# A gated recurrence and a highway layer on one core: short units at both ends of the token loop, and the weight loads moved on ScalarE's queue

## The chip, the cores and the metric

The kernel runs on one NeuronCore of a Trainium2 chip. The metric is the device time of one execution in microseconds, as the median of repeated runs. Besides these there is one profiled execution, whose trace gives the start and the duration of every instruction; its own time is a little different from the median.

## What is computed

A recurrence over 6336 tokens for each of 4 batches and 256 channels, and then a highway layer on each of the 25344 resulting rows (everything float32 in memory):

```python
sig = 1 / (1 + exp(-f_logit))
f = lower_bound + (1 - lower_bound) * sig
for t in range(S):                       # B, S, D = 4, 6336, 256
    h = f[:, t] * h + (1 - f[:, t]) * x[:, t]
    y[:, t] = h
H = maximum(y @ w_h, 0)
T = sigmoid(y @ w_t + b_t)
out = T * H + (1 - T) * y
```

The kernel writes u = sigmoid(-f_logit) and cc = 1 - lower_bound. Then 1 - f = cc * u and f = 1 - cc * u. The scan runs on u * x without the factor cc, and cc is put back into the weights (scaled rows) and into a diagonal matrix used for the output.

## The kernel before

**Units.** Tokens are cut into units, and the kernel is a software pipeline over them. 6336 = 6 x 1024 + 192. Unit 0 holds the first 192 tokens of all four batches: 8 blocks of 96 tokens on 96 partitions (`rest // 2`), so 768 columns. Units 1 to 24 each hold 1024 tokens of one batch, 8 blocks of 128, going round the four batches for each stretch of 1024. `units` (L48 to L51) lists them, and `load` (L67), `gate` (L116), `halves` (L166) and `o_act` (L227) read their sizes.

**Stages of a unit n.** There are two halves h (or m) of 128 channels, and the steps are made for each:

- `load`: logits into `lt`, x into `xt`, both on SP's queue. Four buffers each.
- `gate` (L119): ScalarE, u = sigmoid(-lt), one instruction for the whole unit.
- `product` (L126): GpSimd, bv = u * x, in pieces of two blocks (128x512). The first piece is told to wait for the e of unit n - 3 on VectorE.
- `decay_pe`, `decay_act` (L136, L144): TensorE transposes u so that channels lie on partitions; ScalarE turns it into f.
- `b_pe` (L150): TensorE transposes bv.
- `scan` (L161): VectorE, y = f * y + bv along the tokens; for unit 0 four scans of 192, one a batch, otherwise one of 1024. The last column is carried on.
- `z_pe`, `t_act` (L175, L183): y @ w_t, then the sigmoid with the bias.
- `g_pe`, `d_dve`, `e_dve` (L190, L199, L206 or L209): y @ (cc w_h - cc I), then d = max(-cc y, .), which is max(H, 0) - h, and e = d * T.
- `o_pe`, `o_act` (L223, L224, L233): y times the diagonal plus e, transposed back to tokens on partitions in groups of four blocks; ScalarE copies each group from PSUM and SP stores it (L237, or L241 for unit 0).

**Order.** The order on every engine is written out by hand: `pin` keeps an instruction in program order on its engine. In iteration n of the loop (L247 to L291) stand the load of unit n + 4, the gate and product of n + 2, the decay of n + 1, the scans of n, t, d and e of n - 1, and the output of n - 2. On VectorE that gives scan(n,0), d(n-1,0), scan(n,1), d(n-1,1), e(n-1). Every PSUM tile (uT, bT, zp, gp, op) has one buffer. Output tiles have two.

**Head.** SP issues the loads of units 0 and 1. ScalarE's queue carries lower_bound and the bias in four small transfers, and then w_h and w_t of 256 KB each (L96, L99), all ahead of its first activation. VectorE makes cc, the scaled weights `w_sb` and the diagonal (L101 to L113) before its first scan.

Of the kernel before, what the change touches and what calls it, by code (L numbers as in the profile page):

```python
# [19 lines left out]
def kernel(  # L20
# [21 lines left out]
    NB = 8  # L42
    out_bsd = out.rearrange("(b s) d -> b s d", b=B)


    rest = S % (NB * P)
    assert rest % 2 == 0 and rest // 2 <= P and B * 2 == NB
    units = [(rest // 2, [(b, 0, b * rest, rest) for b in range(B)])]  # L48
    for s0 in range(rest, S, NB * P):
        for b in range(B):  # L50
            units.append((P, [(b, s0, 0, NB * P)]))  # L51
# [14 lines left out]

    def load(n):  # L67
        np_, segs = units[n]
        lt = inp.tile([P, NB, D], FP32, tag="lt")
        xt = inp.tile([P, NB, D], FP32, tag="xt")  # L70
        for src, t in ((f_logit, lt), (x, xt)):
            if len(segs) == 1:
                b, s0, _, ln = segs[0]
                pin(nc.sync.dma_start(t, src[b, s0:s0 + ln, :].rearrange("(j p) d -> p j d", p=np_)))
            else:
                t4 = t.rearrange("p (b j) d -> p b j d", j=2)
                for j in range(2):
                    nc.sync.dma_start(
                        t4[:np_, :, j, :],
                        src[:, j * np_:(j + 1) * np_, :].rearrange("b p d -> p b d"))  # L80
        st[n]["lt"], st[n]["xt"] = lt, xt

    load(0)
# [7 lines left out]
    lb = singles.tile([P, NH], FP32, name="lb")  # L91
    bt = singles.tile([P, NH], FP32, name="bt")
    w_raw = singles.tile([P, 2, NH, D], FP32, name="w_raw")
    for h in range(NH):
        for vec, t in ((lower_bound, lb), (moe_b_t, bt)):
            nc.scalar.dma_start(t[:, h:h + 1], bass.AP(  # L96
                tensor=vec.tensor, offset=vec.offset + h * P, ap=[[1, P], [1, 1]]))
    for k, w in enumerate((moe_w_h, moe_w_t)):
        nc.scalar.dma_start(w_raw[:, k], w.rearrange("(h p) o -> p h o", p=P))  # L99
# [7 lines left out]
    for h in range(NH):  # L107
        for k in range(2):
            nc.vector.tensor_scalar(w_sb[:, k, h], w_raw[:, k, h], cc[:, h:h + 1], None, op0=ALU.mult)
        nc.vector.tensor_scalar(diag[:, h], ident_h, cc[:, h:h + 1], None, op0=ALU.mult)  # L110
        nc.vector.tensor_scalar(ndiag[:, h], ident_h, ncc[:, h:h + 1], None, op0=ALU.mult)

        nc.vector.scalar_tensor_tensor(w_sb[:, 0, h, h * P:(h + 1) * P], w_raw[:, 0, h, h * P:(h + 1) * P],  # L113
                                       cc[:, h:h + 1], ndiag[:, h], op0=ALU.mult, op1=ALU.add)

    def gate(n):  # L116
        np_, _ = units[n]
        u = inp.tile([P, NB, D], FP16, tag="u")
        pin(nc.scalar.activation(u[:np_], st[n]["lt"][:np_], AF.Sigmoid, scale=-1.0))  # L119
        st[n]["u"] = u  # L120

    def product(n, after):
        np_, _ = units[n]
        bv = mid.tile([P, NB, D], BF16, tag="bv")
        for q in range(0, NB, 2):
            ins = pin(nc.gpsimd.tensor_mul(bv[:np_, q:q + 2], st[n]["u"][:np_, q:q + 2], st[n]["xt"][:np_, q:q + 2]))  # L126
            if q == 0 and after is not None:
                tc.add_manual_dep(ins.ins, after.ins.name, mybir.DependencyInfo(
                    mybir.DependencyClass.Sync, mybir.DependencyReason.DATA), reason="shared port")
        st[n]["bv"] = bv  # L130

    def decay_pe(n, h):
        np_, _ = units[n]
        uT = ps1.tile([P, NB * P], FP16, tag="uT")
        for j in range(NB):
            pin(nc.tensor.transpose(uT[:, j * np_:(j + 1) * np_], st[n]["u"][:np_, j, h * P:(h + 1) * P], ident_h[:np_, :np_]))  # L136
        st[n]["uT"] = uT

    def decay_act(n, h):
        np_, _ = units[n]  # L140
        N = NB * np_
        if h == 0:
            st[n]["f"] = mid.tile([P, NH, NB * P], FP16, tag="f", name="f")
        pin(nc.scalar.activation(st[n]["f"][:, h, :N], st[n]["uT"][:, :N], AF.Identity, scale=ncc[:, h:h + 1], bias=1.0))  # L144

    def b_pe(n, h):
        np_, _ = units[n]
        bT = ps1.tile([P, NB * P], BF16, tag="bT")
        for j in range(NB):
            pin(nc.tensor.transpose(bT[:, j * np_:(j + 1) * np_], st[n]["bv"][:np_, j, h * P:(h + 1) * P], ident_b[:np_, :np_]))  # L150
        st[n]["bT"] = bT
# [3 lines left out]
    def scan(n, h):  # L155
        if h == 0:
            st[n]["y"] = ypool.tile([P, NH, NB * P], BF16, tag="y", name="y")
        y = st[n]["y"]
        for b, _, c0, ln in units[n][1]:
            prev = carry.get((b, h))  # L160
            pin(nc.vector.tensor_tensor_scan(  # L161
                y[:, h, c0:c0 + ln], st[n]["f"][:, h, c0:c0 + ln], st[n]["bT"][:, c0:c0 + ln],
                0.0 if prev is None else prev, op0=ALU.mult, op1=ALU.add))
            carry[b, h] = y[:, h, c0 + ln - 1:c0 + ln]

    def halves(n):  # L166
        N = NB * units[n][0]
        return [(0, N // 2), (N // 2, N)]

    def z_pe(n, m):  # L170
        zp = ps1.tile([P, 2, 512], FP32, tag="zp")
        y = st[n]["y"]
        for ki in range(NH):
            for i, (a, e) in enumerate(halves(n)):
                pin(nc.tensor.matmul(zp[:, i, :e - a], w_sb[:, 1, ki, m * P:(m + 1) * P], y[:, ki, a:e],  # L175
                                 start=ki == 0, stop=ki == NH - 1))
        st[n]["zp"] = zp

    def t_act(n, m):
        w = NB * units[n][0] // 2  # L180
        if m == 0:
            st[n]["t"] = ffn.tile([P, NH, 2, 512], BF16, tag="t", name="t")
        pin(nc.scalar.activation(st[n]["t"][:, m, :, :w], st[n]["zp"][:, :, :w], AF.Sigmoid, bias=bt[:, m:m + 1]))  # L183

    def g_pe(n, m):
        gp = ps1.tile([P, 2, 512], FP32, tag="gp")
        y = st[n]["y"]
        for ki in range(NH):
            for i, (a, e) in enumerate(halves(n)):
                pin(nc.tensor.matmul(gp[:, i, :e - a], w_sb[:, 0, ki, m * P:(m + 1) * P], y[:, ki, a:e],  # L190
                                 start=ki == 0, stop=ki == NH - 1))
        st[n]["gp"] = gp

    def d_dve(n, m):
        w = NB * units[n][0] // 2
        if m == 0:
            st[n]["d"] = ffn.tile([P, NH, 2, 512], BF16, tag="d", name="d")
        y2 = st[n]["y"][:, m, :2 * w].rearrange("p (i w) -> p i w", i=2)
        pin(nc.vector.scalar_tensor_tensor(st[n]["d"][:, m, :, :w], y2, ncc[:, m:m + 1], st[n]["gp"][:, :, :w],  # L199
                                       op0=ALU.mult, op1=ALU.max))  # L200

    def e_dve(n):
        w = NB * units[n][0] // 2
        e = mid.tile([P, NH, 2, 512], BF16, tag="e", name="e")
        if w == 512:
            ins = pin(nc.vector.tensor_mul(e, st[n]["d"], st[n]["t"]))  # L206
        else:
            for m in range(NH):
                ins = pin(nc.vector.tensor_mul(e[:, m, :, :w], st[n]["d"][:, m, :, :w], st[n]["t"][:, m, :, :w]))  # L209
        st[n]["e"] = e  # L210
        return ins

    def o_pe(n, q):
        np_, _ = units[n]
        w = NB * np_ // 2
        op = ps1.tile([P, NB // 2, D], FP32, tag="op")
        y, e = st[n]["y"], st[n]["e"]
        for jj in range(NB // 2):
            j = q * (NB // 2) + jj
            i, c = divmod(j * np_, w)  # L220
            for h in range(NH):
                o = op[:np_, jj, h * P:(h + 1) * P]
                pin(nc.tensor.matmul(o, y[:, h, j * np_:(j + 1) * np_], diag[:, h], start=True, stop=False))  # L223
                pin(nc.tensor.matmul(o, e[:, h, i, c:c + np_], ident_b, start=False, stop=True))  # L224
        st[n]["op"] = op

    def o_act(n, q):  # L227
        np_, segs = units[n]
        if q == 0:
            st[n]["o"] = outp.tile([P, NB, D], FP32, tag="o", name="o")  # L230
        o = st[n]["o"]
        oq = o[:, q * (NB // 2):(q + 1) * (NB // 2)]
        pin(nc.scalar.copy(oq[:np_], st[n]["op"][:np_]))  # L233
        if len(segs) == 1:
            b, s0, _, ln = segs[0]
            a = s0 + q * (ln // 2)
            nc.sync.dma_start(out_bsd[b, a:a + ln // 2, :].rearrange("(j p) d -> p j d", p=np_), oq)  # L237
        elif q == 1:
            o4 = o.rearrange("p (b j) d -> p b j d", j=2)
            for j in range(2):  # L240
                nc.sync.dma_start(out_bsd[:, j * np_:(j + 1) * np_, :].rearrange("b p d -> p b d"),  # L241
                                  o4[:np_, :, j, :])
# [4 lines left out]
    for n in range(-3, NU + 2):  # L247
# [21 lines left out]
        if ok(n):  # L269
            scan(n, 1)  # L270
        if ok(n - 1):
# [3 lines left out]
        if ok(n - 2):  # L275
# [44 lines left out]
```

## Time and profile before

| quantity | us |
|---|---|
| median of three runs (lowest, highest) | 236.33 (235.71, 237.41) |
| the profiled run | 237.56 |
| its span, first to last instruction | 235.8 |
| first scan starts | 16.48 |
| first scan of unit 2 starts | 31.65 |
| last e ends | 226.78 |
| last copy of output ends | 231.90 |

Busy time of the engines in that span: VectorE 203.6 us (86%), ScalarE 198.3 (84%), TensorE 192.1 (81%), GpSimd 114.2 (48%). 78.68 MB were moved, 334 GB/s over the span.

How to read it: the page cuts the span into 40 slices and gives the busy tenths of each engine in each. The timeline gives instructions with their start, their duration and, in brackets, the idle time of the engine just before and what ended it. The chain of waits follows back from the last instruction what released what. A share of busy time is a mean over the head, the middle and the tail, which have different limits; it is the stage that has to be read.

### The profile page before, as it was taken

To read this page: it belongs to the slowest core of one execution; us is meant where nothing else is said; L and a number is where in the kernel's file an instruction comes from. 1 tells how busy PE (TensorE), PEld (TensorE's weight loads), DVE (VectorE), ACT (ScalarE), POOL (GpSimd) and SP (SyncE) were. 2 spreads that over 40 slices of the span, in tenths; PEclk is the share of its full clock that TensorE was granted. 3 is DMA by queue.
4 is the path that set the end of the run, shared out by engine and by line. 5 is a ranking of instruction groups with operands and counts; after the bars stand their busy time and mean duration, and the time that the engine had idled before them with its cause. 6 is when DMAs were issued, how large, how long until landed. Compare 5 with 4: busy or idle time off the path is not lost.

```text
span 235.8 us, 4853 instructions
## 1 busy us (share of the span) xinstructions
PE 192.1 (81%) x2000; PEld 134.5 (57%) x2000; DVE 203.6 (86%) x144; ACT 198.3 (84%) x176; POOL 114.2 (48%) x108
## 2 busy tenths in 40 slices
PE   0135899898999989899998989898999989897751
PEld 0125566666566666667566666656666666665441
DVE  0425799999999999999999999999999999999540
ACT  0645789999999999999999999999999999975541
POOL 1088553574376357436634753673475357430000
PEclk9999999999999999999999999999999999999985
DMA  6999999999999999999999999999999995243255
GB/s 150 302 386 386 386 383 386 379 385 383 382 386 383 386 382 386 384 384 379 386 386 382 385 383 383 379 382 375 385 383 386 388 368 205 97 152 119 89 178 177
DMA packets 78805, 78.68 MB, mean 334 GB/s; under 512 B 2240, under 2 KB 78784, under 8 KB 78784
## 3 DMA queue, kind: packets, MB, share of 16 engines
q1 hardware_dynamic: 77664, 77.86, 94.4%
q10 hardware_dynamic: 1120, 0.53, 0.9%
q8 instruction: 15, 0.25, 0.4%
q14 instruction: 6, 0.05, 0.0%
HBM read 52.43 MB, written 25.95 MB: 332 GB/s over the span
## 4 chain that ended last, share of the span: by engine, by line
DVE 77%; issue 6%; PE 5%; ACT 2%; DVEq 0%; ACTq 0%
DVE y L161 45%; DVE d L199 20%; DVE e L206 12%; PE zp L175 1%; PE gp L190 1%; ACT o L233 1%; ACT t L183 1%; PE op L224 1%; PE op L223 1%; PE bT L150 0%; PE uT L136 0%; DVE e L209 0%; DVEq L206 0%; ACTq L233 0%; DVEq L209 0%
## 5 line engine op out<-in xcount | busy, mean ns | idle before, releaser
L126 POOL TENSOR_TENSOR bv<-u,xt 128x512 bf16<-128x512 f16 (+1 forms) x100 | 113.2, 1164 | 93.7 <-DVE e L206 72.9
L161 DVE TENSOR_TENSOR_SCAN y<-f,y,bT 128x1024 bf16<-128x1024 f16 x48 | 112.3, 2341 | 2.6 <-ACT t L183 1.4
L183 ACT ACTIVATE t<-zp,bt 128x1024 bf16<-128x1024 f32 (+1 forms) x50 | 55.3, 1106 | 13.6 <-PE zp L175 10.6
L199 DVE SCALAR_TENSOR_TENSOR d<-y,ncc,gp 128x1024 bf16<-128x1024 bf16 (+1 forms) x50 | 62.2, 1244 | 2.5 <-PE gp L190 2.5
L144 ACT ACTIVATE f<-uT,ncc 128x1024 f16<-128x1024 f16 (+1 forms) x50 | 55.9, 1117 | 5.5 <-PE uT L136 5.5
L233 ACT COPY o<-op 128x1024 f32<-128x1024 f32 (+1 forms) x50 | 50.2, 1005 | 5.7 <-PE op L224 5.7
L190 PE MATMUL gp<-y,w_sb 128*128 128x512 bf16 (+1 forms) x200 | 51.5, 380 | 4.0 <-DVE d L199 1.4
L223 PE MATMUL op<-diag,y 128*128 128x128 f16 (+1 forms) x400 | 50.9, 221 | 2.2 <-ACT o L233 2.2
L175 PE MATMUL zp<-y,w_sb 128*128 128x512 bf16 (+1 forms) x200 | 51.6, 381 | 0.3 <-ACT t L183 0.3
L224 PE MATMUL op<-ident_b,e 128*128 128x128 bf16 (+1 forms) x400 | 50.8, 221 | 0.5 <-DVE e L206 0.5
L119 ACT ACTIVATE u<-lt 128x2048 f16<-128x2048 f32 (+1 forms) x25 | 47.5, 1902 | 2.1 <-DMA lt<-in_f_logit_dram 2.1
L150 PE MATMUL bT<-ident_b,bv 128*128 128x128 bf16 (+1 forms) x400 | 31.7, 222 | 20.8 <-DVE y L161 16.5
L224 PEld LDWEIGHTS <-e 128*128 128x128 bf16 (+1 forms) x400 | 39.7, 100 | 8.8 <-DVE e L206 1.9
L223 PEld LDWEIGHTS <-y 128*128 128x128 bf16 (+1 forms) x400 | 39.8, 100 | 5.7
L150 PEld LDWEIGHTS <-bv 128*128 128x128 bf16 (+1 forms) x400 | 26.8, 99 | 27.5 <-issue 20.0
L136 PE MATMUL uT<-ident_h,u 128*128 128x128 f16 (+1 forms) x400 | 32.2, 227 | 11.0 <-ACT u L119 10.0
L190 PEld LDWEIGHTS <-w_sb 128*128 128x128 f16 x200 | 19.6, 98 | 24.4 <-issue 7.1
L136 PEld LDWEIGHTS <-u 128*128 128x128 f16 (+1 forms) x400 | 26.0, 103 | 11.4 <-ACT u L119 10.0
L206 DVE TENSOR_TENSOR e<-d,t 128x2048 bf16<-128x2048 bf16 x24 | 29.4, 1225 | 2.9 <-DVE d L199 0.5
L175 PEld LDWEIGHTS <-w_sb 128*128 128x128 f16 x200 | 18.7, 99 | 18.2 <-issue 1.1
L161 DVE TENSOR_TENSOR_SCAN y<-f,bT 128x192 bf16<-128x192 f16 x8 | 3.8, 534 | 7.3 <-PE bT L150 7.3
L119 ACT ACT_TABLE_LOAD x1 | 1.3, 1283 | 6.7 <-DMA lt<-in_f_logit_dram 6.7
(15 smaller groups left out, 5.7 us busy)
## 6 DMA issues: line engine op xcount, KB each, us to landing
lt<-in_f_logit_dram SPq DMA_DIRECT2D x24, 1024.0 KB, 9.3
xt<-in_x_dram SPq DMA_DIRECT2D x24, 1024.0 KB, 10.6
out_dram<-o SPq DMA_DIRECT2D x48, 512.0 KB, 7.9
lt<-in_f_logit_dram SPq DMA_DIRECT2D x2, 384.0 KB, 5.0
xt<-in_x_dram SPq DMA_DIRECT2D x2, 384.0 KB, 5.7
out_dram<-o SPq DMA_DIRECT2D x2, 384.0 KB, 6.6
w_raw<-in_moe_w_h_dram ACTq DMA_DIRECT2D x1, 256.0 KB, 4.8
w_raw<-in_moe_w_t_dram ACTq DMA_DIRECT2D x1, 256.0 KB, 5.4
```

The source lines that it names most:

```text
L126: ins = pin(nc.gpsimd.tensor_mul(bv[:np_, q:q + 2], st[n]["u"][:np_, q:q + 2], st[n]["xt"][:np_, q:q + 2]))
L136: pin(nc.tensor.transpose(uT[:, j * np_:(j + 1) * np_], st[n]["u"][:np_, j, h * P:(h + 1) * P], ident_h[:np_, :np_]))
L144: pin(nc.scalar.activation(st[n]["f"][:, h, :N], st[n]["uT"][:, :N], AF.Identity, scale=ncc[:, h:h + 1], bias=1.0))
L150: pin(nc.tensor.transpose(bT[:, j * np_:(j + 1) * np_], st[n]["bv"][:np_, j, h * P:(h + 1) * P], ident_b[:np_, :np_]))
L161: pin(nc.vector.tensor_tensor_scan(y[:, h, c0:c0 + ln], st[n]["f"][:, h, c0:c0 + ln], st[n]["bT"][:, c0:c0 + ln], 0.0 if prev is None else ...
L175: pin(nc.tensor.matmul(zp[:, i, :e - a], w_sb[:, 1, ki, m * P:(m + 1) * P], y[:, ki, a:e], start=ki == 0, stop=ki == NH - 1))
L183: pin(nc.scalar.activation(st[n]["t"][:, m, :, :w], st[n]["zp"][:, :, :w], AF.Sigmoid, bias=bt[:, m:m + 1]))
L190: pin(nc.tensor.matmul(gp[:, i, :e - a], w_sb[:, 0, ki, m * P:(m + 1) * P], y[:, ki, a:e], start=ki == 0, stop=ki == NH - 1))
L199: pin(nc.vector.scalar_tensor_tensor(st[n]["d"][:, m, :, :w], y2, ncc[:, m:m + 1], st[n]["gp"][:, :, :w], op0=ALU.mult, op1=ALU.max))
L206: ins = pin(nc.vector.tensor_mul(e, st[n]["d"], st[n]["t"]))
L223: pin(nc.tensor.matmul(o, y[:, h, j * np_:(j + 1) * np_], diag[:, h], start=True, stop=False))
L224: pin(nc.tensor.matmul(o, e[:, h, i, c:c + np_], ident_b, start=False, stop=True))
```

## The change

The list of units has other sizes. The first 192 tokens become two units of two batches each: 4 blocks of 96 tokens on 96 partitions, 384 columns, two scans of 192 for each half. The first 1024 tokens of batch 0 become two units of 512, and the last 1024 tokens of batch 3 become units of 512, 256 and 256. There are 29 units in place of 25, of which 22 have 1024 tokens. Every stage takes the number of blocks from the unit. A unit with up to four blocks has one output group.

On the head: a one-column sigmoid on a zeroed tile stands ahead of everything on ScalarE. lower_bound is one transfer. The two weight loads (w_t first) and the bias are issued on ScalarE's queue behind the gate of unit 0. The scaling of the weights on VectorE stands behind the two scans of unit 0, as one instruction for both matrices of a half, plus the one that subtracts the diagonal. The diagonals are still made at the start.

```diff
+    FIRST, LAST = (4, 4), (4, 2, 2)
...
-    units = [(rest // 2, [(b, 0, b * rest, rest) for b in range(B)])]
+    for b in range(0, B, 2):
+        units.append((rest // 2, 4, [(b, 0, rest), (b + 1, rest, rest)], slice(b, b + 2), 0))
     for s0 in range(rest, S, NB * P):
         for b in range(B):
-            units.append((P, [(b, s0, 0, NB * P)]))
+            last = s0 + NB * P == S and b == B - 1
+            a = s0
+            for nb in (LAST if last else FIRST if not b and s0 == rest else (NB,)):
+                units.append((P, nb, [(b, 0, nb * P)], b, a))
+                a += nb * P
...
+    def pieces(n, dram, t, j0, j1):
+
+        np_, nb, _, b, a = units[n]
+        if isinstance(b, int):
+            return [(dram[b, a + j0 * P:a + j1 * P, :].rearrange("(j p) d -> p j d", p=P), t[:, j0:j1])]
+        t4 = t[:np_, :nb].rearrange("p (b j) d -> p b j d", j=2)
+        return [(dram[b, a + j * np_:a + (j + 1) * np_, :].rearrange("b p d -> p b d"), t4[:, :, j]) for j in range(2)]
...
+    warm = singles.tile([P, 1], FP32, name="warm")
+    nc.gpsimd.memset(warm, 0.0)
+    nc.scalar.activation(warm, warm, AF.Sigmoid)
+
+    lb = singles.tile([P, NH], FP32, name="lb")
+    bt = singles.tile([P, NH], FP32, name="bt")
+    w_raw = singles.tile([P, 2, NH, D], FP32, name="w_raw")
+    nc.scalar.dma_start(lb, lower_bound.rearrange("(h p) -> p h", p=P))
     load(0)
     load(1)
...
-    for h in range(NH):
-        for vec, t in ((lower_bound, lb), (moe_b_t, bt)):
-            nc.scalar.dma_start(t[:, h:h + 1], bass.AP(
-                tensor=vec.tensor, offset=vec.offset + h * P, ap=[[1, P], [1, 1]]))
-    for k, w in enumerate((moe_w_h, moe_w_t)):
-        nc.scalar.dma_start(w_raw[:, k], w.rearrange("(h p) o -> p h o", p=P))
...
+    def load_weights():
+        for k, w in enumerate((moe_w_t, moe_w_h)):
+            pin(nc.scalar.dma_start(w_raw[:, 1 - k], w.rearrange("(h p) o -> p h o", p=P)))
+        pin(nc.scalar.dma_start(bt, moe_b_t.rearrange("(h p) -> p h", p=P)))
+
+    def weights():
+        for h in range(NH):
+            pin(nc.vector.tensor_scalar(w_sb[:, :, h], w_raw[:, :, h], cc[:, h:h + 1], None, op0=ALU.mult))
+
+            pin(nc.vector.scalar_tensor_tensor(
+                w_sb[:, 0, h, h * P:(h + 1) * P], w_raw[:, 0, h, h * P:(h + 1) * P], cc[:, h:h + 1], ndiag[:, h],
+                op0=ALU.mult, op1=ALU.add))
...
+    def spans(n):
+        N = units[n][0] * units[n][1]
+        return [(a, min(a + 512, N)) for a in range(0, N, 512)]
...
         if ok(n):
             scan(n, 1)
+        if n == 0:
+            weights()
         if ok(n - 1):
             g_pe(n - 1, 1)
         if ok(n + 2):
             gate(n + 2)
-        if ok(n - 2):
+        if n + 2 == 0:
+            load_weights()
+        if ok(n - 2) and units[n - 2][1] > QB:
             o_pe(n - 2, 1)
             o_act(n - 2, 1)
```

`QB` is half of `NB`, 4 blocks. In the functions left out, the fixed 8 blocks are replaced by the unit's own number and the fixed halves of a unit by pieces of up to 512 columns.

## The prediction

> **What bounds the kernel now.** First the page's slices: where an engine is full, and where it is not.
>
> ```profile
> PE   0135899898999989899998989898999989897751
> ...
> DVE  0425799999999999999999999999999999999540
> ACT  0645789999999999999999999999999999975541
> ...
> GB/s 150 302 386 386 386 383 386 379 385 383 382 386 383 386 382 386 384 384 379 386 386 382 385 383 383 379 382 375 385 383 386 388 368 205 97 152 119 89 178 177
> ```
>
> VectorE is full from about the sixth slice (5.9 us each) to the third from the end. Two things are not full: the head and the tail. The data rate stands at 375 to 388 GB/s in nearly the whole middle. The windows of the trace give the stages (start:end, then length, busy us of PE, PE weight loads, DVE, ACT, POOL, PE clock, DMA share, GB/s):
>
> ```profile
> 0.00:31.65 31.65, 13.14 (x108) 9.54 (x109) 13.93 (x26) 16.13 (x13) 14.64 (x20) 1.00 1.01 326
> 31.65:211.01 179.36, 164.74 (x1760) 115.39 (x1758) 176.69 (x110) 171.22 (x154) 99.60 (x88) 1.00 1.02 360
> ...
> 220.34:231.90 11.56, 7.46 (x76) 5.33 (x73) 3.78 (x4) 6.17 (x6) 0.00 (x0) 0.84 0.46 163
> 231.90:235.80 3.90, 0.00 (x0) 0.00 (x0) 0.00 (x0) 0.00 (x1) 0.00 (x0) 0.50 0.38 134
> ```
>
> In the middle VectorE is busy 98.5% (176.69 of 179.36). The chain of waits says the same: one period holds both scans, both d, one e, and no other engine.
>
> ```profile
> 162.74 2.26 DVE y L161
> 165.00 0.72 DVE d L199
> 165.72 0.36 issue
> 166.09 2.34 DVE y L161
> 168.43 1.18 DVE d L199
> 169.70 1.23 DVE e L206
> 170.93 2.26 DVE y L161
> ```
>
> Scan to scan is 8.19 us a unit. The scan at 31.65 us is unit 2's first; the e that ends at 220.34 is unit 23's: 23 periods, 188.7 us, 8.20 each. The span is **31.65 head + 188.7 packed VectorE + 11.6 last hand-offs + 3.9 last store = 235.8**. The profiled run took 237.56, so 1.76 lie outside the span; it is 1.2 above the median of 236.33.
>
> Transfers are a near second: a unit moves two loads and a store of 1024 x 256 x 4 bytes, 3.146 MB, and in 8.2 us that is 384 GB/s. They have a lead, though. Unit 22's logits are issued at 164.09 and land about 9.3 later (median of their row), and their gate is at 183.95: 10.5 us of slack.
>
> The head in the timeline:
>
> ```profile
> 6.71 1.28 ACT L119 ACT_TABLE_LOAD   x1 [6.71 <-DMA lt<-in_f_logit_dram]
> ...
> 11.46 4.52 POOL L126 TENSOR_TENSOR bv<-u,xt 96x512 bf16<-96x512 f16 x4 [9.80 <-DMA xt<-in_x_dram]
> ...
> 16.48 1.89 DVE L161 TENSOR_TENSOR_SCAN y<-f,bT 128x192 bf16<-128x192 f16 x4 [5.92 <-PE bT L150]
> ```
>
> The logits land at 6.71, the table is loaded only then, x lands at 11.46, the product takes 4.52, and the first scan is at 16.48. x is late because SP issues it only at 4.68: the waits of SP's queue show 3.0 us for lower_bound, which x does not need. [...]
>
> [...] eight 128-column transposes take 1.01 us at 18 to 23 us, 0.61 from 26.8; at 228 to 230 the clock is back at 0.54. [...] the two weight loads on ScalarE's queue land 4.8 and 5.4 us after issue while SP's queue is loaded. [...]
>
> **The change, part by part.**
>
> *Work of VectorE.* Elements are the same. Instructions rise: scans 56 to 62, d 50 to 58, e 26 to 29. A line through the shapes (scan 2341 at 1024; d 1255 and 988 at 1024 and 768; e 1225 at 2048, 551 at 768) gives a fixed part of 0.1 to 0.2, of which 0.08 to 0.1 overlaps the neighbour: d's 8 extra cost about 1 us, the others nothing to speak of. They lie in head and tail, counted there.
>
> *Middle.* The 22 remaining whole units run the same instructions in the same order: 22 x 8.20 = 180.4. Cover for this zero is the 10.5 us lead of the loads.
>
> *Table load hoisted:* 1.28 off the first gate. *lower_bound* is one issue in place of two; the bias moves behind the weights. *Weights* go behind gate(0) on ScalarE's queue: three issues of about 0.5 each (row of L99: 0.46 and 0.49), with f(0,0) behind them, which waits for transposes anyhow. On VectorE the scaling moves from idle time at 7.6 to 10.6 to between scan(0,1) and scan(1,0): 2 x 0.62 + 2 x 0.35 less overlap, about 1.4, now on the path of the head.
>
> *SP's queue* issues 62 loads and 53 stores in place of 52 and 50, about 0.5 each; its waits (58.6 us for ScalarE's o alone) cover that. The first six transfers (logits 0, x 0, logits 1) go without a wait; x 1 waits for lower_bound (landed 4.66 before) and logits 0; unit 2's wait for x 0 and logits 1; **x of unit 3 waits for w_t**, and all later loads stand behind it.
>
> *Head, step by step.* Half the logits (0.39 MB of 0.79) land at about 5.0: before, the windows have 0.39 MB moved by 4.1 us, and landing lags by about 1. gate(0) 1.05 (1.90 at 2048 with 0.2 fixed), to 6.1. x 0 lands at about 6.5. Product 2 x 1.16, to 8.9. Transposes 0.4, scan(0,0) at 9.3 (16.48 before). The second half follows through f and the bank it frees, scan(0,1) ends near 11.9. Weights: triggers at 6.1 and 6.6, plus 5.4: landed 11.5 to 12.0. Scaling to 13.4. From here I set every instruction down in its engine's order, each starting when its engine is free and its inputs and its one PSUM bank are, with the rows' durations and cold matmuls. After the scaling come scan(1,0), 0.93, and on PE g and z of unit 0, cold, 1.4, to 14.9; z(0,1) waits until t has emptied the bank, g(0,1) stands behind it, and so d(0,1) at 17.2, to 17.8; g and z of unit 1, 1.3; sixteen cold output matmuls 1.9, to 21.0; ScalarE's o 1.0, f 0.6, t 0.5, then the gate of unit 4 1.9, to 25.0; its product 4.6, to 29.7; e(2) and transposes, and **scan(4,0) at 31.0**. The same setting-down for the kernel before puts scan(2,0) at 32.3 where the trace has 31.65. So scan(4,0), the same tokens as unit 2 before, is only 0.65 earlier: all the early start is spent on a pipeline of six short iterations whose hand-offs, not elements, take the time. But less is left behind it: d and e of a 512 unit, 1.9, where before a 1024's 3.5 stood.
>
> *From scan(4,0) to the end of e(25):* 180.4 + 1.9 (d, e of unit 3) + 2.2 (scans of unit 26) = 184.5, end at 215.5, against 220.34.
>
> *Tail.* After it: scans of 27 and 28 (4 x 0.55), d and e of 26 (1.9), 27 and 28 (2 x 1.05): 6.2 of work. ScalarE has t, f and seven copies, about 8. Set down in order, with VectorE waiting some 3 us for g and t, the last e ends at 225.2. Then eight output matmuls 0.6 and one 512-column copy 0.6: 226.5. Before, two groups of 16 and two 1.0 copies, the second at half clock, took 5.1 from the last e. I add 0.4 for a half clock in the new tail: 226.9. The last store is 256 KB in place of 512: [...]
>
> Sum: 226.9 + 3.3 = 230.2 against 235.8, **5.6 less**. On the median: **230.7 us**.
>
> *Bounds of what the trace does not show.* Head: if PE is warm from about 16 us, scan(4,0) comes at 28.5; not earlier, since ScalarE's copy of unit 2's output needs unit 0's store out of the buffer, and it queues behind some 10 MB of loads. If landing is as late as before (6.7) or the weights take 7 us, 33. A loss beyond that is rival 3. Tail from e(25): 8 us (work plus one hand-off) to 13 (cold PE throughout); I take 11.4.
>
> **Rivals.**
> 1. *The head gains nothing*: the 96-row loads are slow (270 GB/s between 8 and 10.5 us before, 386 afterwards) and scan(4,0) comes at 33: 2.0 later than forecast, 232.7. For it: PE is cold there. Against: slack of gate(2) to its landing is over 1 us in my setting-down.
> 2. *Head as in 1, and a cold, hand-off-bound tail of 13*: 234.3, or up to 236 with a late store; within 1%. For it: every short unit has its full ring of hand-offs (g, d, e, op, o), each with one buffer. Against: before's tail already ran cold at its end.
> 3. *Late weights, slower*: scaling stands ahead of scan(1,0), and x 3 with all later loads behind w_t. Each us of landing past 12 is one us lost. It eats the gain at 17.6 and is over 1% slower from 20; at 21, 239.7. For it: triggers wait for logits 0 and its gate, and compete with 3.1 MB from SP. Against: [...] even served last, behind 3.7 MB at 386 GB/s, they land near 14.
> 4. *The change does not shorten anything*: the DMA rate bounds, head and tail only move idle time. It would need the 10.5 us lead to vanish: 236.3. Against: the rate falls off at 194, 41 us ahead of the end.
>
> **How the numbers follow.** Forecast 0.60 (228.3 to 232), rival 1 0.20, rival 2 0.10, rival 4 0.03, rival 3 0.07. About 1% (2.4 us) is what can be told from no change: faster below 233.97. Forecast and rival 1 and a little of 2: 0.83; same 0.11; slower 0.06. Range: 228 (warm head) to 234.3 (rival 2); what lies past either end is below 2 in 10.
>
> **What would show it.** First scan near 9.3; first 1024 scan near 31; 22 periods of 8.20; last e near 225 and 1.5 to 2 us to the last copy; last store 3.3. It is wrong if the period moves, if gates wait for DMA in the middle, or if the scaling ends past 14.

## The result, and the profile after

The changed kernel takes **239.94 us** (median of four runs, 239.72 to 240.24), the kernel before 236.13 beside it. The ratio is 1.0153, 95% interval 1.0111 to 1.0194: 1.5% slower, where 2.4% faster was forecast. The profiled run's span is 238.2 us (before 235.8).

The page's slices after the change, to be laid beside those of before:

```profile
DVE  1389882699999999999999999998999999999971
...
GB/s 173 275 348 348 348 355 358 361 367 364 358 361 370 360 361 373 367 363 371 372 363 366 377 361 362 375 361 360 370 366 361 372 372 377 312 159 118 176 206 146
```

The head and the tail did what they were meant to do: the first scan starts at 8.91 us (16.48 before), VectorE stands at 8 or 9 from the third to the sixth slice (before: 2, 5, 7 and 9), and it works up to the last slice but one. Two things are new. VectorE has a hole in the seventh and eighth slices. And the rate is 348 GB/s in the third to fifth slices, where it was 386, and 355 to 377 in the middle, where it was 375 to 388, although the same bytes are moved (78.69 MB, 78.68 before) in packets of the same size (on SP's queue 77.86 MB in 77872 packets, before in 77664: 1.0 KB each).

The chain of waits of the page says what carries the end. First the kernel before, then the changed one:

```profile
DVE 77%; issue 6%; PE 5%; ACT 2%; DVEq 0%; ACTq 0%
```

```profile
DMA 51%; DVE 24%; PE 11%; ACT 5%; issue 4%; POOL 2%; SPq 0%; ACTq 0%; DVEq 0%; POOLq 0%
DMA out_dram<-o 42%; DVE y L178 14%; DMA xt<-in_x_dram 7%; DVE d L213 7%; DVE e L219 4%; ACT o L242 3%; PE zp L191 2%; POOL bv L142 2%; PE gp L205 2%; PE op L232 2%; PE op L233 2%; ACT f L160 2%; DMA lt<-in_f_logit_dram 1%; PE uT L152 1%; ACT t L199 1%
```

Before, VectorE stood for 77% of it. Now the stores stand for 42%. A store is on the chain only where somebody waits for it, and the list of waits (engine and line, whom it waited for, us in total, times, longest) names ScalarE's copy of the output, which needs a free output buffer:

```profile
ACT o L242 <- DMA out_dram<-o: 14.4, 11, 6.6
...
PE op L232 <- ACT o L242: 7.8, 10, 1.0
...
DVE e L219 <- ACT t L199: 6.7, 6, 5.2
```

In the kernel before this wait does not occur once. The longest is in the head, in ScalarE's timeline:

```profile
30.11 0.68 ACT L199 ACTIVATE t<-zp,bt 128x512 bf16<-128x512 f32 x1
37.36 1.01 ACT L242 COPY o<-op 128x1024 f32<-128x1024 f32 x1 [6.57 <-DMA out_dram<-o]
38.27 1.12 ACT L160 ACTIVATE f<-uT,ncc 128x1024 f16<-128x1024 f16 x1
39.28 0.69 ACT L199 ACTIVATE t<-zp,bt 128x512 bf16<-128x512 f32 x1
```

The copy at 37.36 is unit 2's, the third to be made, and there are two output buffers. Unit 0's copy ended at 20.6. SP issues its store only at 27.44. The two loads of unit 6 still stand in front of it in SP's order, and every load of 1 MB issued since 11.80 has held the queue for about 2.8 us or more:

```profile
17.62 2.87 SPq L88 DMA_DIRECT2D xt<-in_x_dram  x1
20.58 2.79 SPq L88 DMA_DIRECT2D lt<-in_f_logit_dram  x1
23.46 3.89 SPq L88 DMA_DIRECT2D xt<-in_x_dram  x1
27.44 3.52 SPq L244 DMA_DIRECT2D out_dram<-o  x2
```

It has left its buffer at about 37.3, where the waiting copy starts. Behind that copy on ScalarE stand f of unit 5 and t of unit 3; behind t, e(3) on VectorE; behind f, the next scans and TensorE. (scan(5,1) is the scan of unit 5, half 1, and so on.) VectorE's timeline shows the idle time (in brackets) that follows:

```profile
34.10 0.72 DVE L213 SCALAR_TENSOR_TENSOR d<-y,ncc,gp 128x512 bf16<-128x512 bf16 x1
40.00 0.69 DVE L219 TENSOR_TENSOR e<-d,t 128x1024 bf16<-128x1024 bf16 x1 [5.17 <-ACT t L199]
40.61 2.34 DVE L178 TENSOR_TENSOR_SCAN y<-f,y,bT 128x1024 bf16<-128x1024 f16 x1
42.86 1.26 DVE L213 SCALAR_TENSOR_TENSOR d<-y,ncc,gp 128x1024 bf16<-128x1024 bf16 x1
46.39 2.35 DVE L178 TENSOR_TENSOR_SCAN y<-f,y,bT 128x1024 bf16<-128x1024 f16 x1 [2.27 <-PE bT L166]
```

The 5.17 us ahead of e(3) end with t, which had stood behind the waiting copy. The 2.27 ahead of scan(5,1), at 46.39, end with a transpose of bv. That bv had long been there: GpSimd made it from 30.46 to 34.97. The transpose is late on TensorE, where it stands behind other work in the order that the program pins:

```profile
39.44 1.01 PE L152 MATMUL uT<-ident_h,u 128*128 128x128 f16 x8 [4.12 <-ACT f L160]
...
41.95 1.91 PE L191 MATMUL zp<-y,w_sb 128*128 128x512 bf16 x4
...
45.68 0.61 PE L166 MATMUL bT<-ident_b,bv 128*128 128x128 bf16 x8
46.07 0.59 PEld L191 LDWEIGHTS <-w_sb 128*128 128x128 f16 x4
46.12 1.03 PE L191 MATMUL zp<-y,w_sb 128*128 128x512 bf16 x4
```

TensorE sat idle for 4.12 us behind f of unit 5, and then the clock granted to it was 0.50 from 40 to 44 us; from 46 to 48 it was 1.00. Four matmuls of the same shape took 1.91 us at 41.95 and 1.03 at 46.12. At the later clock two such groups, g and z of unit 4, would have been 1.8 us shorter (an estimate from these figures), and scan(5,1) waited 2.27. So the wait for one buffer shows twice: once as a wait, and once more as slow work after it. That the idle time brought the lower clock is the author's reading of that order of events and was not tried by itself; with a third output buffer (e12) the clock was 1.00 from 40 to 100 us, and here 0.96.

The sum, against the forecast's own steps, from the timelines. scan(4,0) is the first scan of a unit of 1024 tokens, e(25) the last e of such a unit. The runs e1, e12 and e5 are experiments below: e1 has the old data rate again, e12 a third output buffer, e5 both. No wait for a store is left in e5; its profiled run is the fastest of its six (228.45, median 230.25).

| stretch | forecast | after | e1 | e12 | e5 |
|---|---|---|---|---|---|
| start to scan(4,0) | 31.0 | 28.74 | 27.83 | 29.23 | 27.63 |
| scan(4,0) to scan(6,0) | - | 22.4 | 19.2 | 16.6 | 15.0 |
| scan(6,0) to the end of e(25) | - | 173.1 | 170.2 | 170.2 | 170.2 |
| scan(4,0) to the end of e(25) | 184.5 | 195.5 | 189.3 | 186.8 | 185.2 |
| end of e(25) to the end of the span | 14.7 | 13.9 | 13.9 | 13.9 | 13.9 |
| span | 230.2 | 238.2 | 231.1 | 229.9 | 226.7 |

Against e5 the changed kernel loses 1.1 us in the first row, 7.4 in the second, behind the first wait, and 2.9 in the third. The other ten waits for stores begin at 110 us, and from 140 us on VectorE's round is 8.5 us in place of 8.19:

```profile
200.01 1.23 DVE L219 TENSOR_TENSOR e<-d,t 128x2048 bf16<-128x2048 bf16 x1
...
208.51 1.23 DVE L219 TENSOR_TENSOR e<-d,t 128x2048 bf16<-128x2048 bf16 x1
```

A unit's 3.146 MB in 8.5 us are 370 GB/s, which is what the slices show there (360 to 377). In this last part of the loop the transfers set the pace, as long as there are two output buffers: in e12, at the same rate, the round stays at 8.19 (e at 200.27 and 208.46).

### The profile page after: what moved, and what is told of

It is laid out like the page before. It is cut to its first block, busy times and chain, and to the rows that moved or that the text cites. A ratio compares the mean times of both kernels' runs of the same rounds, so it can differ in the third digit from the quotient of the medians.

```text
span 238.2 us, 4951 instructions
## 1 busy us (share of the span) xinstructions
PE 195.4 (82%) x2008; PEld 134.5 (56%) x2008; DVE 209.0 (88%) x159; ACT 200.4 (84%) x198; POOL 114.4 (48%) x109
## 2 busy tenths in 40 slices
DMA packets 78981, 78.69 MB, mean 330 GB/s; under 512 B 2416, under 2 KB 78960, under 8 KB 78960
## 3 DMA queue, kind: packets, MB, share of 16 engines
q1 hardware_dynamic: 77872, 77.86, 98.0%
## 4 chain that ended last, share of the span: by engine, by line
DMA 51%; DVE 24%; PE 11%; ACT 5%; issue 4%; POOL 2%; SPq 0%; ACTq 0%; DVEq 0%; POOLq 0%
DMA out_dram<-o 42%; DVE y L178 14%; DMA xt<-in_x_dram 7%; DVE d L213 7%; DVE e L219 4%; ACT o L242 3%; PE zp L191 2%; POOL bv L142 2%; PE gp L205 2%; PE op L232 2%; PE op L233 2%; ACT f L160 2%; DMA lt<-in_f_logit_dram 1%; PE uT L152 1%; ACT t L199 1%
## 5 line engine op out<-in xcount | busy, mean ns | idle before, releaser
L178 DVE TENSOR_TENSOR_SCAN y<-f,y,bT 128x1024 bf16<-128x1024 f16 (+2 forms) x54 | 113.7, 2106 | 5.3 <-PE bT L166 5.1
L242 ACT COPY o<-op 128x1024 f32<-128x1024 f32 (+2 forms) x51 | 50.8, 996 | 19.2 <-DMA out_dram<-o 14.4
L213 DVE SCALAR_TENSOR_TENSOR d<-y,ncc,gp 128x1024 bf16<-128x1024 bf16 (+3 forms) x58 | 63.9, 1101 | 1.4 <-PE gp L205 1.3
L199 ACT ACTIVATE t<-zp,bt 128x1024 bf16<-128x1024 f32 (+3 forms) x58 | 57.7, 996 | 7.6 <-PE zp L191 6.6
L160 ACT ACTIVATE f<-uT,ncc 128x1024 f16<-128x1024 f16 (+3 forms) x58 | 58.1, 1002 | 1.5 <-PE uT L152 1.4
L205 PE MATMUL gp<-y,w_sb 128*128 128x512 bf16 (+2 forms) x204 | 53.8, 381 | 3.4 <-DVE d L213 1.7
L191 PE MATMUL zp<-y,w_sb 128*128 128x512 bf16 (+2 forms) x204 | 53.7, 381 | 0.0
L135 ACT ACTIVATE u<-lt 128x2048 f16<-128x2048 f32 (+3 forms) x29 | 48.7, 1679 | 5.2 <-DMA lt<-in_f_logit_dram 5.2
L166 PE MATMUL bT<-ident_b,bv 128*128 128x128 bf16 (+1 forms) x400 | 33.3, 222 | 16.1 <-DVE y L178 12.0
L232 PEld LDWEIGHTS <-y 128*128 128x128 bf16 (+1 forms) x400 | 39.7, 100 | 5.8 <-issue 0.3
L219 DVE TENSOR_TENSOR e<-d,t 128x2048 bf16<-128x2048 bf16 (+3 forms) x29 | 32.0, 1104 | 9.1 <-ACT t L199 6.7
L166 PEld LDWEIGHTS <-bv 128*128 128x128 bf16 (+1 forms) x400 | 26.3, 99 | 22.6 <-issue 14.7
```

The source lines that it names most:

```text
L178: pin(nc.vector.tensor_tensor_scan(y[:, h, c0:c0 + ln], st[n]["f"][:, h, c0:c0 + ln], st[n]["bT"][:, c0:c0 + ln], 0.0 if prev is None else ...
L191: pin(nc.tensor.matmul(zp[:, a:e], w_sb[:, 1, ki, m * P:(m + 1) * P], st[n]["y"][:, ki, a:e], start=ki == 0, stop=ki == NH - 1))
L199: pin(nc.scalar.activation(st[n]["t"][:, m, :N], st[n]["zp"][:, :N], AF.Sigmoid, bias=bt[:, m:m + 1]))
L205: pin(nc.tensor.matmul(gp[:, a:e], w_sb[:, 0, ki, m * P:(m + 1) * P], st[n]["y"][:, ki, a:e], start=ki == 0, stop=ki == NH - 1))
L213: pin(nc.vector.scalar_tensor_tensor(st[n]["d"][:, m, :N], st[n]["y"][:, m, :N], ncc[:, m:m + 1], st[n]["gp"][:, :N], op0=ALU.mult, op1=AL ...
L242: pin(nc.scalar.copy(o[:np_, j0:j1], st[n]["op"][:np_, :j1 - j0]))
```

## The experiments

**Why is the rate lower?** One line of the change has nothing to do with units. The tile `warm` has one column of 4 bytes, and it takes 32 bytes of every partition. Buffers are placed one after the other, so everything behind it moves: in the built programs `lt` begins at byte 24832 before (97 x 256) and at 24864 after, and all `lt`, `xt` and `o` buffers are 32 bytes past a multiple of 256. The rival is the traffic itself: 115 transfers in place of 102, smaller ones, in another order.

*e1*, the changed kernel with a wider `warm`:

```diff
-    warm = singles.tile([P, 1], FP32, name="warm")
+    warm = singles.tile([P, 64], FP32, name="warm")[:, 0:1]
```

> The changed kernel with its one-column tile `warm` made 64 columns (256 bytes a partition) wide, nothing else. Address theory (the 32 bytes of `warm` put every load and store buffer 32 bytes past a 256-byte boundary, and that slows the transfers): the rate of 346 to 350 GB/s between 11 and 30 us goes back to about 386, the copies of ScalarE no longer wait 14 us for stores, and the time falls to 229 to 233 us. Traffic theory (more and smaller transfers and another order of them slow the DMA, wherever the buffers lie): the rate stays near 348 and the time near 240.

Measured: 233.45 us, ratio to before 0.9835 (0.9792 to 0.9879), half a microsecond above the range. The slices, and the copy of unit 2's output:

```profile
DVE  1399886799999999999999999999999999999971
...
GB/s 176 299 386 386 383 385 385 383 387 381 382 384 372 384 380 383 382 386 382 385 385 382 386 382 386 384 379 381 374 377 380 381 366 299 187 183 94 182 224 139
```

```profile
34.24 1.01 ACT L242 COPY o<-op 128x1024 f32<-128x1024 f32 x1 [4.36 <-DMA out_dram<-o]
```

*e2*, the kernel before, with 32 unused bytes and nothing else:

```diff
+    pad = singles.tile([P, 8], FP32, name="pad")
+    nc.gpsimd.memset(pad, 0.0)
     load(0)
```

> The kernel before with an unused tile of 32 bytes a partition ahead of its other tiles, so that every load and store buffer moves up by 32 bytes; no other edit. Address theory: the rate in the head falls from 386 to about 348 GB/s, the 10.5 us lead of the loads is used up before the end, and the time rises by 3 to 8 us, to 239 to 244. Traffic theory: within 1% of 236.1, rate 386.

Measured: 244.46 us (up to 244 expected), ratio 1.0309 (1.0256 to 1.0361); between 11 and 30 us 345 GB/s (before 386). Its chain of waits changes as that of the changed kernel did:

```profile
GB/s 139 272 348 348 348 348 348 354 365 373 362 364 373 370 362 370 374 364 364 375 365 363 373 370 358 364 374 360 364 371 366 363 369 375 155 173 174 90 173 173
...
DMA 67%; DVE 8%; ACT 6%; PE 5%; issue 3%; ACTq 0%; SPq 0%; DVEq 0%
DMA out_dram<-o 67%; DVE y L163 4%; ACT o L235 3%; ACT t L185 3%; DVE d L201 3%; PE gp L192 2%; PE zp L177 1%; DVE e L208 1%; ACT f L146 1%; PE op L225 1%; PE op L226 1%; PE bT L152 0%; PE uT L138 0%; DVE e L211 0%; ACTq L235 0%
```

The traffic theory falls twice: the new traffic runs at 386 GB/s once the address is right, and the old traffic at 345 once it is wrong. *e3* and *e10* are e2 with 16 and 32 columns in `pad`, 64 and 128 bytes.

> As e2, but 64 bytes. Address theory, if a boundary of 256 bytes is what counts: as slow as e2 (239 to 244). If one of 64 bytes counts: within 1% of 236.1 and a rate of 386. Traffic theory: within 1% too.

> As e2 and e3, with 128 bytes. If a start on a multiple of 256 is what counts: about 243 us and 348 GB/s in the head, as with 32 and 64. If 128 is enough: within 1% of before and 386.

Measured: e3 242.97, ratio 1.0237 (1.0194 to 1.0281); e10 241.70, ratio 1.0175 (1.0119 to 1.0231); both run at 348 GB/s in the third to fifth slices. So with loads alone the three shifts tried short of 256 (32, 64 and 128) cost the same tenth (345, 343 and 346 GB/s between 11 and 30 us, before 386), and 256, in e1, costs nothing (385). When stores run beside the loads, from 40 to 100 us, the shift by 32 reaches 365 GB/s, that by 64 368 and that by 128 372, and the times fall in the same order; why is open.

*e4* takes `warm` out altogether.

```diff
-    warm = singles.tile([P, 1], FP32, name="warm")
-    nc.gpsimd.memset(warm, 0.0)
-    nc.scalar.activation(warm, warm, AF.Sigmoid)
```

> The changed kernel without the tile `warm`, its memset and its activation: the buffers lie where they lay before, and the table load of 1.28 us stands ahead of the first gate again. Address theory: 386 GB/s, and 0 to 1.3 us above e1, 230 to 234. Traffic theory: 240 to 241.

Measured: 232.85, ratio 0.9806 (0.9761 to 0.9850), not to be told from e1. The early table load, for which the tile was there, is worth nothing that can be measured; without it the logits land at 4.4 us and the table load of 1.28 follows, so that the first gate starts at 5.67 us (4.63 in the changed kernel), but the copy of unit 2's output, which waits for its buffer, starts at 34.12 in e4 and at 34.24 in e1.

**Loads or stores?** *e8* puts an unused tile into the pool of the output buffers, so that they alone move, by 64 bytes; *e9* moves the load buffers by 32 and brings the output buffers back (u, which lies in the pool of the load buffers, moves with them).

```diff
+    pad = outp.tile([P, 8], FP32, name="pad")        # e8
...
+    pad = singles.tile([P, 8], FP32, name="pad")     # e9
+    pad2 = mid.tile([P, 40], FP32, name="pad2")
```

> The kernel before with an unused tile in the pool of the output buffers, so that only the two output buffers move, by 64 bytes a partition; the load buffers stay on multiples of 256. If the shift slows stores as it slows loads: the rate of the middle falls below 380 GB/s and the time rises by 1 to 4 us. If only loads, which write to the on-chip memory, are slowed: within 1% of before, rate 380 to 386 in the middle.

> The kernel before with the load buffers 32 bytes past a multiple of 256 and the output buffers brought back onto one by a second unused tile. If loads alone carry the loss (stores shifted by themselves cost nothing in e8): head rate about 348 GB/s and 242 to 245.5 us, as in e2. If it takes both, or if it is their distance from each other: clearly below e2, under 240.

Measured: e8 237.53, ratio 0.9996 (0.9969 to 1.0023), 384 GB/s from 40 to 100 us; e9 244.46, ratio 1.0297 (1.0240 to 1.0354). The rates, e8 first:

```profile
GB/s 146 303 386 386 386 383 386 383 386 384 381 385 381 386 381 384 383 385 380 386 384 383 385 382 381 381 386 376 380 381 385 386 367 195 98 152 118 93 181 170
```

```profile
GB/s 139 262 348 348 348 346 348 352 367 374 360 364 373 369 362 372 372 363 366 376 364 363 374 369 362 367 371 362 362 372 366 363 370 373 179 173 175 89 173 173
```

With the stores alone shifted, by 64 bytes, nothing is lost, and with the loads alone shifted, by 32, all of e2's loss is there: 348 GB/s in the third to fifth slices, 386 in e8. At the shifts tried, only the loads, which write into the on-chip memory, mind where they begin.

**What does the low rate hold up?** Three output buffers in place of two, in the kernel of e1 (*e5*) and in the changed kernel as it is (*e12*):

```diff
-    outp = ctx.enter_context(tc.tile_pool(name="outp", bufs=2))
+    outp = ctx.enter_context(tc.tile_pool(name="outp", bufs=3))
```

> The kernel of e1 with three output buffers in place of two. In e1 ScalarE's copy of unit 2's output waits 4.4 us (29.9 to 34.2) until unit 0's store has left its buffer. If that wait is what keeps e1 above the forecast (4.4 us gained against before, 5.6 forecast): the wait is gone, the second 1024 scan comes near 34 in place of 37.5, and the time falls by 2 to 4 us to about 230. Rival: the loads are late next (they queue behind the same data), ScalarE's gates then wait for logits, and less than 1 us is gained.

> The changed kernel as it is, buffers 32 bytes off, with three output buffers. If the transfer rate bounds it: the copies' waits for stores shrink, but logits or x come late instead, and the time stays within 2 us of 240. If it was only the two output buffers that the slower stores blocked: 231 to 234 at the low rate.

Measured: e5 **230.25**, ratio 0.9687 (0.9630 to 0.9744), the lowest time. e12 231.47, ratio 0.9750 (0.9689 to 0.9812): its buffers are 32 bytes off, and it is faster than before all the same. The two intervals overlap, so with three output buffers the low rate costs little or nothing that can be told. The slices of e12 and its waits for transfers:

```profile
DVE  1288869999999999999999999999999999999971
...
GB/s 168 282 349 348 346 349 363 360 366 357 358 376 367 360 372 370 360 374 367 361 375 366 363 370 368 358 371 364 362 373 367 363 371 369 375 381 294 184 229 136
```

```profile
POOL bv L142 <- DMA xt<-in_x_dram: 14.5, 4, 4.7
...
ACT u L135 <- DMA lt<-in_f_logit_dram: 4.3, 3, 2.1
...
ACT o L242 <- DMA out_dram<-o: 3.1, 4, 0.9
```

The second branch of that expectation came true, and that is the most telling result. At 366 GB/s a unit's 3.146 MB take 8.6 us and VectorE's round 8.19, yet VectorE stays at 9 from the seventh slice to the 38th, and from scan(6,0) to the end of e(25) e12 needs 170.2 us like e5. What lags is not lost: the loads have their lead, the stores a third buffer to queue in, and they catch up in the 35th and 36th slices, at 375 and 381 GB/s, where the changed kernel had 312 and 159. So in this loop the second output buffer runs out before the lead of the loads does.

The cover is finite, though. The lag is, as an estimate from these figures, 0.4 us a unit, some 9 us over the 22 whole units. The four waits for stores in e12 begin at 171 us and grow from 0.4 to 0.9 us, just before the loop ends. A longer loop was not run.

**What are the splits worth?** *e6* and *e7* are e1 without the split at the end and at the head; *e11* is e5 without the one at the head.

```diff
-    FIRST, LAST = (4, 4), (4, 2, 2)
+    FIRST, LAST = (4, 4), (NB,)        # e6
+    FIRST, LAST = (NB,), (4, 2, 2)     # e7, e11
```

> The kernel of e1 with the last 1024 tokens as one unit. Forecast's reading (tail split is worth about 3 us: smaller last groups, copy and store): 2 to 4 us above e1, 235.5 to 237.5. Rival (hand-offs of the short units eat what they save): within 1 us of e1.

> The kernel of e1 with the first 1024 tokens of batch 0 as one unit (the two units of 384 columns stay). If the 512 units shorten the head: 1 to 3 us above e1. If they only bring the output copy to its wait for the store earlier: within 1 us of e1 or below it, with a shorter wait of ScalarE's copy for stores.

> The kernel of e5 (aligned, three output buffers) with the first 1024 tokens of batch 0 as one unit. In e7 the split at the head was worth nothing, but there two output buffers cost some 9 us of waits of ScalarE's copies. If the split matters once the stores are out of the way: 1 to 3 us above e5, 231.5 to 233. If hand-offs eat it: within 1 us of e5 (230.25).

Measured: e6 234.85, ratio 0.9922 (0.9898 to 0.9947) against 0.9835 of e1: the split at the end is worth 0.9%, some 2 us. e7 232.34, ratio 0.9782 (0.9727 to 0.9838): with two output buffers the split at the head is worth nothing that can be told. e11 232.57, ratio 0.9813 (0.9763 to 0.9863) against 0.9687 of e5: with three it is worth 1.3%, some 3 us. With two buffers a head that gets further sooner only meets the busy buffer sooner: in e1 one copy waits 4.4 us for a store, at 29.9 us; in e7 the first wait comes at 39.7, and there are 13 of them, 8.8 us in all.

## Why the prediction was wrong, step by step

*The middle* is the step that failed: "Cover for this zero is the 10.5 us lead of the loads." From scan(4,0) to the end of e(25) 184.5 us were forecast and 195.5 measured. It failed in two terms, and the loss needs both: with the old rate alone (e1) the kernel gains 1.7%, with a third output buffer alone (e12) 2.5%, with both (e5) 3.1%.

The first term: the rate of 386 GB/s was taken over unchanged. The edit that changed it was priced, under "Table load hoisted", at 1.28 us gained; that its tile moves the addresses of all load buffers was not looked at, though the list of addresses of the built program would have shown it. The runs show the loss for loads: 346 to 349 GB/s in the third to fifth slices at 32, 64 and 128 bytes past a multiple of 256, in place of 383 to 386 on one. The stores, which read from the shifted buffers, lost nothing at 64 bytes (e8: 384 GB/s from 40 to 100 us, before 384). What in a load costs the tenth no run here shows.

The second term: the lead of the *loads* was weighed, and the *stores* have none. They have two buffers. The prediction named the very wait ("ScalarE's copy of unit 2's output needs unit 0's store out of the buffer") but used it only as a floor for how early scan(4,0) could come. It acts on the instructions behind it instead: 6.6 us in the changed kernel, and still 4.4 in e1, where the addresses are right. That is why e1 gains 1.7% and not the 2.4% forecast. One reading belongs to it: the prediction has SP issue a transfer in "about 0.5 each", but in the trace of before the 1 MB loads from 11.34 to 27.70 us hold SP's queue for 2.55 to 3.04 us each (2.8 and more after), and a store has to wait behind them. One of them, in the kernel before:

```profile
19.70 2.56 SPq L74 DMA_DIRECT2D lt<-in_f_logit_dram  x1
```

*Head*: right, and a little cautious. First scan forecast at 9.3, measured 8.91; weights landed 6.0 and 6.4 us after issue (forecast 5.4). The scaling ended at 14.2 (13.4), past the 14 that the prediction named as a sign of being wrong; it cost nothing that shows, since scan(4,0) came at 28.74 (31.0). The prediction's "cold" and "warm" PE are the 1.01 and 0.61 us that it read for eight transposes. Four of them took 0.56 at 17.42 and 0.39 at 19.39 in the changed kernel, so the short times came between, near the case of its early bound (warm from about 16, scan(4,0) at 28.5).

*Tail*: forecast 14.7 from the end of e(25), measured 13.9 in the changed kernel, e1, e12 and e5 alike; from the last e to the last copy 1.3 us (forecast 1.5 to 2), the last store 3.0 (the 3.3 in the sum was the author's estimate; the store of 512 KB before took 3.9). Two terms nearly cancel here, which is luck: scans of 256 tokens took 0.74 each (0.55), and VectorE waited 2.0 us for g, t and transposes (3).

*Period*: it stayed at 8.19 as long as nothing waited for a store (scans at 83.92, 92.10 and 100.29 in the changed kernel) and moved to 8.5 from 140 us on, which the prediction had named as a sign of being wrong. Rival 3's late weights did not happen: x of unit 3 did wait for w_t, as forecast, but SP's queue stood only 1.6 us for it. Rival 4, the transfers as the bound, came nearest, and for the last part of the loop it holds. But it looked for the gates to wait for loads, and those waited 5.2 us in all, in the head; the stores were what ran out.

## What to carry to other kernels

A new small tile ahead of the load buffers is an edit to every load behind it (here a tile of 32 bytes a partition, and 386 GB/s became 348): compare the addresses of the buffers, and see the rate in the first load-only stretch of the profile, before anything else is explained. When a head is made to run ahead, ask which buffer it returns to first; here it was the output buffer, whose store was queued on the same queue behind the loads. A rate below the demand need not cost time as long as every stream has somewhere to queue (e12: 366 GB/s, where a unit of 3.146 MB in 8.19 us asks for 384, and the round stayed at 8.19): reckon the lag per round times the rounds, and compare it with the lead and the buffers.

## What the runs showed that was not expected

- Loads that begin 32, 64 or 128 bytes past a multiple of 256 run at 346 to 349 GB/s in the third to fifth slices, those on it at 383 to 386; stores shifted by 64 bytes do not change the rate (384 from 40 to 100 us, before 384).
- A wait of 6.6 us on ScalarE left TensorE idle for 4.12 us, and after it the granted clock was 0.50 from 40 to 44 us, 0.73 from 44 to 46 and 1.00 from 46 to 48; four matmuls took 1.91 us at 41.95 and 1.03 at 46.12.
- e of a 512 unit took 1.70 us at 27.12 in the changed kernel and 0.69 at 40.00. During the first GpSimd's product ran (23.74 to 28.27), during the second it did not. The order by hand keeps the product away from the e three units earlier, and in the short iterations it meets another. The same holds for the two scaling instructions, 1.45 at 11.61 beside a product (10.51 to 12.78) and 0.48 at 13.36 after it. That GpSimd is the cause was not tried.
